# Sigmoid-gated layer behind routed attention: the values of the last batch in seven products of quarters

## The chip, the cores and the metric

The kernel runs on one core of a Trainium2 chip. The time is the device time of one execution in microseconds (us). Before the change the median of three runs is 320.71 us (320.22 to 320.73).

The engines go by the names of the profile: PE (TensorE, matrix products, with PEld for its weight loads), ACT (ScalarE), DVE (VectorE), POOL (GpSimd) and SP (the queue that issues most transfers). Each works off its own instructions in the order in which the program wrote them and waits at an instruction until what that one needs is there.

## The reference

Attention with routing, and then a gated layer on its output:

```python
mask = q_assign[:, :, :, None] == k_assign[:, :, None, :]
scores = np.where(mask, scale * np.matmul(q, k.transpose(0, 1, 3, 2)), -1000000000.0)
attn = np.exp(scores - np.max(scores, axis=-1, keepdims=True))
attn = attn / (np.sum(attn, axis=-1, keepdims=True) + 1e-09)
x = np.matmul(attn, v)                      # 4 batches, 8 heads, 768 tokens, 64
...                                         # heads side by side: 3072 x 512
gate = 1.0 / (1.0 + np.exp(-(x @ w_gate)))  # 512 x 1536
val = x @ w_val                             # 512 x 1536
out = gate * val @ w_out                    # 1536 x 512
```

q and k are assigned to the nearest of 16 centroids per head. Everything comes and goes as float32; the products run in float16 with float32 sums.

## The kernel before

**Attention.** The four batches follow each other. Each batch has 96 steps; a step is one product of scores (`sc`, line 1026), one exponential on ACT (`es`, 1031) and three small products with the values (`av`, 1049). The step counter runs from 0 to 383, and the last batch begins at step 288. A table `SCHED` gives for many small pieces of work the step at which they are written into the program. Between two steps `ffn_run` fills PE with the gated layer of the batch before, taken from a queue. So the layer of the last batch has no attention left to lie beside, and runs alone behind it: this is the stage that the change is about.

**Half inputs.** The attention puts 2.0 where the sum of the weights is formed, so the tile `xT` holds x / 2, transposed: four chunks of 128 columns (the contraction) by 768 tokens. With it, `1 + tanh(g)` is twice the sigmoid and the value group `v` is half of the value, and `(th + 1) * v` (line 643) is the gated value `hT`.

**Columns and blocks.** The 1536 columns of the layer are 12 groups of 128 (`fc`), the tokens of a batch two blocks of 384. A plain group (`fin_group`, 622) is four matmuls, one for each chunk.

**The last batch: `closing` (from line 646).** The groups 0 and 1 are plain, gate and value. The other ten are taken in pairs, by a `Unit` for each pair. For its gates a Unit doesn't compute four plain groups (two columns by two blocks, 16 matmuls) but seven products of quarters of two matmuls each (14): `p1` to `p7`. They need differences of the gate's weights (`fin_weights`, 602, eight of them, written at the steps in `SCHED["fw"]`) and of the tokens (`fin_tokens`, 616). Two PSUM banks hold the running sums of a Unit. `x` takes p1, then p6, p7 and p4 on top; after each of them ACT copies its state out (`c1` 693, `c12` 701, `c22` 710, and the tanh of `c21` 718). `y` takes p5 and later p3. DVE adds what is missing (`plus`, 650): p2 to `c1`, `y` to `c22`, and `y` with p3 to `c12`. ACT then takes the tanh in place (711, 719, 726). The next product into `x` cannot begin before the copy of the state before is done. The values of all ten groups are plain: four groups for each pair, 16 matmuls, and on DVE line 643 after each. They are written between the products of the next pair.

The order in `closing` is written out by hand in the list `seq`, and each engine keeps to it. Four PSUM banks are a pool called `ring` (plain groups and p2); a new tile gets the bank that was given back first. The pools `op` and `avp` have two banks each, for `x` and `y`. The second operands of the layer (`Sums.make`, 869 to 875) are sums over `hT` on DVE, and the tail of the stage is the output product, also by seven products (`pair`, 763), and its stores.

Of the kernel before, what the change touches and what calls it, by code (L numbers as in the profile page):

```python
# [8 lines left out]
FP = mybir.dt.float32  # L9
# [86 lines left out]
}  # L96


# [1 line left out]
def kernel(  # L100
# [61 lines left out]
    def bank(n=512, dt=FP, name="bank"):  # L162
        return ring.tile([128, n], dt, tag="ring", name=name)
# [3 lines left out]
    def out_bank():  # L167
        taken["op"] += 1
        return op.tile([128, DM], FP, tag="o", name="o")
# [225 lines left out]
    T = {}  # L395
# [187 lines left out]
                        "p (h x) -> p h x", h=2  # L583
                    )

    def fin_weights(i, t):

        fin_room()
        a = FC0 // 2 if i == 0 else 0
        q = lambda k, j: wg[i][:, 2 * k : 2 * k + 2].rearrange(  # L590
            "p d (q j) f -> p d q j f", j=2
        )[:, :, a:, j]
        tw = lambda t: fin["kq"[i], (t - 1) // 2][:, (t - 1) % 2].rearrange(
            "p (d q f) -> p d q f", d=2, q=3
        )
        fin["T", i, t] = tw(t)
# [5 lines left out]
        DVE.tensor_tensor(cut(z), cut(x), cut(y), ALU.subtract)  # L602
# [25 lines left out]
    def fin_plain(xT, fc, blk):  # L628
        b, st = B - 1, []

        def gate():
            if fc == 0:
                need(*(("x", b, p, 3 * blk + c) for p in range(NP) for c in range(3)))
                HB[b, blk] = htp.tile([128, NFC, 384], HP, name="hT")
            g = fin_group(xT, 0, fc, blk)
            st.append(thp.tile([128, 384], FP, name="th"))
            ACT.activation(st[0], g, AF.Tanh)

        return [(NDC * 163, gate), (NDC * 163, lambda: hidden(xT, fc, blk, st[0]))]

    def hidden(xT, fc, blk, th):
        w = fin_group(xT, 1, fc, blk)
        DVE.scalar_tensor_tensor(HB[B - 1, blk][:, fc], th, 1.0, w, ALU.add, ALU.mult)  # L643

    def closing(xT):

# [1 line left out]

        b = B - 1
        plus = lambda dst, a, z: DVE.tensor_tensor(dst, a, z, ALU.add)  # L650
        fin_tokens(xT, 4)
        room = [tp.tile([128, 12, 128], HP, tag="T", name="T") for _ in range(7)]
        slot = []
        for t in room[:4]:
# [4 lines left out]
        for m, n in ((m0, 0), (ma, 0), (mb, 1)):  # L659
            for i in (1, 2, 3):  # L660
                if n == 0:
                    m.of[i] = sump.tile([128, HF, 128], HP, tag="sum", name="sum")
                else:
                    m.of[i] = room[4 + i // 2][:, HF * (i % 2) : HF * (i % 2) + HF]
        m0.of[4], ma.of[4], mb.of[4] = room[4][:, 0:HF], room[6][:, 0:HF], room[6][:, HF:12]

        class Unit:
            def __init__(u, n, f):
                u.f, u.i, u.q = f, f // WQ, f % WQ // 2
                n = n % 2  # L670
                u.c1, u.c12, u.c22, u.c21 = slot[4 * n : 4 * n + 4]

            def mm(u, o, k, start, stop):
                T_ = lambda t, d: fin["T", u.i, t][:, d, u.q, :]
                W_ = lambda k_, j, d: wg[u.i][:, 2 * k_ + d, (u.f + j) % WQ, :]
                A_ = lambda i, k_, d: xT[:, 2 * k_ + d, 384 * (1 - i) : 384 * (2 - i)]
                S_ = lambda t, d: fin["S", t][:, d]
                for d in range(2):
                    l, r = {
                        1: lambda: (W_(0, 0, d), A_(0, 0, d)), 2: lambda: (W_(1, 0, d), A_(0, 1, d)),  # L680
                        3: lambda: (W_(1, 1, d), S_(4, d)), 4: lambda: (T_(4, d), A_(1, 1, d)),
                        5: lambda: (T_(1, d), S_(1, d)), 6: lambda: (T_(2, d), S_(2, d)),
                        7: lambda: (T_(3, d), S_(3, d)),
                    }[k]()
                    PE.matmul(  # L685
                        out=o, lhsT=l, rhs=r, start=start and d == 0, stop=stop and d == 1,
                        skip_group_check=True,
                    )

            def p1(u):  # L690
                u.x = out_bank()[:, 0:384]
                u.mm(u.x, 1, True, True)
                ACT.activation(u.c1, u.x, AF.Copy)

            def p5(u):
                u.y = avp.tile([128, 512], FP, tag="av", name="av")[:, 0:384]
                u.mm(u.y, 5, True, True)

            def p6(u):
                u.mm(u.x, 6, False, True)  # L700
                ACT.activation(u.c12, u.x, AF.Copy)

            def p2(u):
                z = bank(512, name="gz")[:, 0:384]
                u.mm(z, 2, True, True)
                plus(u.c1, z, u.c1)

            def p7(u):
                u.mm(u.x, 7, False, True)
                ACT.activation(u.c22, u.x, AF.Copy)  # L710
                ACT.activation(u.c1, u.c1, AF.Tanh)

            def sum22(u):
                plus(u.c22, u.y, u.c22)

            def p4(u):
                u.mm(u.x, 4, False, True)
                ACT.activation(u.c21, u.x, AF.Tanh)
                ACT.activation(u.c22, u.c22, AF.Tanh)

            def p3(u):
                u.mm(u.y, 3, False, True)
                plus(u.c12, u.y, u.c12)

            def tanh12(u):
                ACT.activation(u.c12, u.c12, AF.Tanh)
# [5 lines left out]
        seq = []  # L732
        units = [Unit(n, f) for n, f in enumerate((6, 2, 8, 4, 10))]
        old = [f for fc in range(FC0) for _, f in fin_plain(xT, fc, 1)]
        def part(i, m, c0, c1, eng=None):
            return lambda: m.make(i, c0, c1, eng)

        extra = {
            3: [part(3, m0, 0, 4), part(3, ma, 0, 4)],
            4: [part(1, m0, 0, 4), part(2, m0, 0, 4)],  # L740
        }
# [62 lines left out]
        u = units[-1]  # L804
        both = lambda m, *c: [part(1, m, *c), part(2, m, *c)]
        seq += [lambda: u.v(0), part(1, ma, 0, 4), u.p3, u.tanh12, p0(1), lambda: u.v(1), part(2, ma, 0, 4), pa(1)]
        seq += [lambda: u.v(2), *both(m0, 4, HF), pb(1), lambda: u.v(3), l0([(0, HD)]), *both(ma, 4, HF)]
        seq += [la([(0, HD)]), part(1, mb, 0, HF), p0(6), part(2, mb, 0, HF), p0(5)]
        seq += [part(3, m0, 4, HF), part(3, ma, 4, HF), pa(6), part(4, m0, 0, HF), pa(5), part(3, mb, 0, HF)]
        seq += [p0(7), part(4, ma, 0, HF), pb(6), part(4, mb, 0, HF), pb(5)]  # L810
        seq += [pa(7), p0(4), p0(3), pb(7), pa(4), pa(3), pb(4), pb(3), lb([(0, HD // 2), (HD // 2, HD)])]
        return [(0.0, f) for f in seq]

    def plain_out(b, blk, t):
# [847 lines left out]
    for b in range(B):  # L1662
        xT = xtp.tile([128, NDC, S], HP, tag="xTb", name="xTb")
        key = min(b, 1)
        for i in range(2 if b else NPT):
            u = BASE[b] + (DONE0[i] if b == 0 else 96 - 12 * halved(b) if i == 0 else 96)
            lag = SCHED.get(f"lag{key}{i}", 8)
            if b == B - 1:
                if i == 0:
                    at(u + lag, lambda xT=xT: queue.extend(a for fc in range(FC0) for a in fin_plain(xT, fc, 0)))  # L1670
                    at(u + SCHED.get("fs1", 9), lambda xT=xT: (fin_tokens(xT, 1), fin_tokens(xT, 2)))
                    at(BASE[b] + 48 + SCHED.get("fs3", 17), lambda xT=xT: fin_tokens(xT, 3))
                    for k, s_ in enumerate(SCHED["fw"]):
                        at(s_, lambda k=k: fin_weights(1 - k // 4, 1 + k % 4))
# [56 lines left out]
```

## Time and profile before

| | |
|---|---|
| median of the runs | 320.71 us |
| the profiled execution | 320.28 us |
| its span, first to last instruction | 318.5 us |
| PE busy over the span | 312.2 us (98%) |
| DVE, ACT, POOL busy | 233.7, 240.4 and 109.0 us |
| first matmul of the last batch's layer | 271.63 us |
| last matmul | 315.15 us |

Times in the views of the profile count from the first instruction. A row of the timeline gives the start, the duration, the engine, the line, the tiles written and read, and in brackets how long the engine was idle before it and what ended that. Matmuls are pipelined: a pair of them is shown with 0.49 us, though the next pair begins 0.33 us after it. A row of a group gives the count, the time in all and the mean of one in ns.

### The profile page before, as it was taken

What the parts mean: (1) busy time and instruction counts of PE and PEld (TensorE: products, weight loads), DVE (VectorE), ACT (ScalarE), POOL (GpSimd) and SP (SyncE); (2) the same over time, 40 slices, a digit from 0 to 9 for tenths busy, and PEclk for the clock granted to TensorE, in tenths of its full rate; (3) what the DMA queues carried; (4) which work ended last, traced back from release to release, by engine and by line L of the source; (5) the groups of instructions that cost most, each with busy time, mean ns of one, the idle gap of its engine ahead of it and who ended that gap; (6) DMA issues with size and microseconds to landing.
All of it is one profiled execution on the core that took longest, in us unless ns stands there. A gap on an engine that the chain in (4) does not pass through costs nothing.

```text
span 318.5 us, 9195 instructions
## 1 busy us (share of the span) xinstructions
PE 312.2 (98%) x3500; PEld 221.1 (69%) x3500; DVE 233.7 (73%) x615; ACT 240.4 (75%) x545; POOL 109.0 (34%) x145
## 2 busy tenths in 40 slices
PE   7999999999999999999999999999999999999995
PEld 5888666766766666666777678666777678666685
DVE  6899656778687777686779678776766777668873
ACT  6688998797889887877767786887878886466521
POOL 5888454244434275423233342523202111000000
PEclk9999999999999999999999999999999999999999
DMA  7999998748859988977775555872612120300014
GB/s 197 374 266 187 262 158 132 180 95 244 243 102 178 188 231 133 204 211 149 110 204 139 180 111 147 255 106 52 112 24 67 42 27 20 138 3 0 1 35 165
DMA packets 77996, 45.16 MB, mean 142 GB/s; under 512 B 56896, under 2 KB 75520, under 8 KB 77952
## 3 DMA queue, kind: packets, MB, share of 16 engines
q1 hardware_dynamic: 73840, 39.66, 51.3%
q0 software_dynamic: 3680, 4.72, 8.9%
q8 instruction: 27, 0.44, 0.6%
q10 hardware_dynamic: 432, 0.20, 0.2%
q14 instruction: 17, 0.14, 0.2%
HBM read 28.34 MB, written 6.29 MB: 109 GB/s over the span
## 4 chain that ended last, share of the span: by engine, by line
PE 95%; DVE 2%; POOL 1%; issue 0%; ACT 0%; POOLq 0%; DVEq 0%
PE sc L1026 19%; PE g L531 15%; PE v L547 15%; PE av L1049 11%; PE o L954 9%; PE v L622 5%; PE o L825 5%; PE lg L435 2%; PE o L685 2%; PE o_end L763 2%; PE lg L422 1%; PE o L763 1%; PE av L763 1%; PE av L685 1%; PE t_ps L1275 1%; PE oh_ps L1335 1%
## 5 line engine op out<-in xcount | busy, mean ns | idle before, releaser
L1031 ACT ACTIVATE es<-sc 128x384 f16<-128x384 f32 x384 | 174.1, 492 | 38.6 <-PE sc L1026 29.9
L1026 PE MATMUL sc<-T 128*128 128x384 f16 x384 | 117.5, 326 | 0.4 <-DVE T L1356 0.4
L1049 PEld LDWEIGHTS <-es 128*128 128x128 f16 x1152 | 81.3, 98 | 35.1 <-ACT es L1031 0.2
L1049 PE MATMUL av<-va,es 128*128 128x65 f16 x1152 | 97.6, 194 | 0.0
L552 DVE SCALAR_TENSOR_TENSOR hT<-th,v 128x384 f16<-128x384 f32 x72 | 39.8, 553 | 38.3 <-PE av L1049 34.1
L531 PE MATMUL g<-xTb,wg 128*128 128x384 f16 x288 | 58.5, 326 | 0.2 <-DVE hT L552 0.2
L547 PE MATMUL v<-xTb,wv 128*128 128x384 f16 x288 | 58.6, 326 | 0.1
L376 POOL TENSOR_TENSOR xp<-t,rec 128x384 f16<-128x384 f32 (+1 forms) x30 | 21.6, 721 | 96.9 <-DVE rec L373 48.1
L537 ACT ACTIVATE th<-g 128x384 f32<-128x384 f32 x72 | 35.4, 491 | 8.7 <-PE g L531 6.7
L531 PEld LDWEIGHTS <-wg 128*128 128x128 f16 x288 | 27.9, 97 | 14.3 <-issue 0.4
L547 PEld LDWEIGHTS <-wv 128*128 128x128 f16 x288 | 28.0, 98 | 13.9 <-issue 0.3
L1026 PEld LDWEIGHTS <-T 128*128 128x128 f16 x384 | 37.1, 97 | 0.7 <-DVE T L1356 0.7
L1592 POOL TENSOR_TENSOR hl<-kraw,hl 128x384 f16<-128x384 f32 x22 | 20.2, 920 | 41.4 <-DVE hl L1591 24.3
L1592 POOL TENSOR_TENSOR hl<-qraw,hl 128x384 f16<-128x384 f32 x22 | 21.2, 962 | 11.1 <-DVE hl L1591 11.1
L825 PE MATMUL o<-wo,hT 128*128 128x512 f16 x72 | 19.9, 379 | 0.0
L371 DVE TENSOR_TENSOR t<-av,sv 128x390 f32<-128x390 f32 (+1 forms) x30 | 14.4, 480 | 7.2 <-PE av L1049 5.2
L622 PE MATMUL v<-xTb,wv 128*128 128x384 f16 x96 | 18.9, 326 | 0.0
L901 DVE TENSOR_TENSOR ob<-o,ob 128x256 f32<-128x256 f32 (+1 forms) x28 | 15.0, 549 | 4.7 <-PE o L954 3.2
L954 PE MATMUL o<-wo,hT 128*128 128x256 f16 x108 | 16.8, 273 | 0.0
L954 PEld LDWEIGHTS <-sum 128*128 128x128 f16 x144 | 14.0, 97 | 3.3
L643 DVE SCALAR_TENSOR_TENSOR hT<-T,v 128x384 f16<-128x384 f32 x20 | 11.0, 552 | 5.3 <-PE v L622 5.3
L450 DVE TENSOR_REDUCE lgs<-lg 128x192 f32<-128x384 f32 x23 | 12.7, 551 | 2.3 <-PE lg L435 2.3
(207 smaller groups left out, 445.2 us busy)
## 6 DMA issues: line engine op xcount, KB each, us to landing
vraw<-in_v_dram SPq DMA_DIRECT2D x15, 384.0 KB, 5.0
kraw<-in_k_dram SPq DMA_DIRECT2D x14, 384.0 KB, 4.9
qraw<-in_q_dram SPq DMA_DIRECT2D x12, 384.0 KB, 4.1
out_dram<-ob SPq DMA_DIRECT2D x17, 256.0 KB, 2.2
wg<-in_moe_w_gate_dram POOLq DMA_DIRECT2D x2, 768.0 KB, 9.6
wv<-in_moe_w_val_dram POOLq DMA_DIRECT2D x2, 768.0 KB, 10.5
wo<-in_moe_w_out_dram POOLq DMA_DIRECT2D x2, 768.0 KB, 9.4
T<-ohT SPq DMA_DIRECT2D x44, 24.0 KB, 1.9
```

Source lines behind the costliest of these rows:

```text
L376: (eng or POOL).tensor_tensor(x, t[:, 0:nq, 0:64], bcast(rec[:, 0:nq], 64), ALU.mult)
L531: PE.matmul(out=g[:, 0:n], lhsT=wg[fc // WQ][:, dc, fc % WQ, :], rhs=xT[:, dc, t0 : t0 + n], start=(dc == 0), stop=(dc == NDC - 1),)
L537: ACT.activation(th[:, 0:n], g[:, 0:n], AF.Tanh)
L547: PE.matmul(out=w[:, 0:n], lhsT=wv[fc // WQ][:, dc, fc % WQ, :], rhs=xT[:, dc, t0 : t0 + n], start=(dc == 0), stop=(dc == NDC - 1),)
L552: DVE.scalar_tensor_tensor(HB[b, blk][:, fc, 0:n], st[0][:, 0:n], 1.0, w[:, 0:n], ALU.add, ALU.mult)
L622: PE.matmul(out=o[:, 0:384], lhsT=w[:, dc, fc % WQ, :], rhs=xT[:, dc, 384 * blk : 384 * blk + 384], start=(dc == 0), stop=(dc == NDC - 1),)
L825: PE.matmul(out=o, lhsT=HB[b, blk][:, fc, bass.ts(t, 128)], rhs=wo[fc // WON][:, fc % WON, :], start=(fc == 0), stop=(fc == NFC - 1),)
L954: PE.matmul(out=st[z][:, e], lhsT=a[:, c, :], rhs=rhs[:, c, :], start=start and c + e == 0, stop=c == HF - 1, skip_group_check=True,)
L1026: PE.matmul(out=sc.rearrange("p (c t) -> p c t", t=128), lhsT=s["k"], rhs=s["q"], start=True, stop=True,)
L1031: ACT.activation(es, sc, AF.Exp, scale=SCALE)
L1049: PE.matmul(out=av[:, a0 + s["c0"] + i, :], lhsT=s["es"][:, bass.ts(i, 128)], rhs=VA[b, p][:, e, s["j"], :], start=(first and i == 0 and a ...
L1592: POOL.tensor_tensor(hl[:, :, 64:128], r, hl[:, :, 0:64], ALU.subtract)
```

## The change

Four of the five pairs get their values by seven products of quarters as well, each between the gates of the next pair (pairs in the order 6, 2, 4, 8, 10; before 6, 2, 8, 4, 10). The values of the last pair, 10, stay plain.

- A value Unit costs 14 matmuls instead of 16. ACT copies its states `c12` and `c22` (times 2), DVE copies `c1` (times 2) and adds with `twice` (2a + z). The gated products of three of its quarters go to POOL (`gated`), the fourth is one DVE instruction straight from PSUM (in `p4`).
- It needs eight differences of the value weights; they are written at steps 328 to 345 into four tiles of the pool `hl`.
- The gates of the last batch are sigmoids of 2g in place of tanh, and the value is multiplied by 2. One instruction at the head of `closing` takes a sigmoid of a single column first. The other batches keep tanh.
- The `y` bank of a Unit comes from `ring` (the first Unit's from `avp`), the `x` of a value Unit from `avp`.
- The gate of `c12` of the pair before is written right behind its `p3`, ahead of `p6`; before, it stood behind `p6`.
- The plain gates and values of groups 0 and 1 in block 0 are now written at the head of `closing`, the token difference 4 behind them.
- The sums for the output products are dealt out anew: fewer beside the Units, more in the tail.

```diff
+    "fwv": [328, 328.5, 331.5, 332, 332.5, 340, 340.5, 345], "END": 0,
...
-            ACT.activation(st[0], g, AF.Tanh)
+            ACT.activation(st[0], g, AF.Sigmoid, scale=2.0)
...
     def hidden(xT, fc, blk, th):
         w = fin_group(xT, 1, fc, blk)
-        DVE.scalar_tensor_tensor(HB[B - 1, blk][:, fc], th, 1.0, w, ALU.add, ALU.mult)
+        DVE.scalar_tensor_tensor(HB[B - 1, blk][:, fc], w, 2.0, th, ALU.mult, ALU.mult)
...
+        twice = lambda dst, a, z: DVE.scalar_tensor_tensor(dst, a, 2.0, z, ALU.mult, ALU.add)
+        ACT.activation(r1, ones[:, 0:1], AF.Sigmoid)
+        first = [f for fc in range(FC0) for _, f in fin_plain(xT, fc, 0)]
+        seq = [*first, lambda: fin_tokens(xT, 4)]
...
+            def copy(u, dst):
+                ACT.activation(dst, u.x, AF.Copy, scale=2.0 if u.w else 1.0)
+
+            def gated(u, j, blk, z, th):
+                POOL.tensor_tensor(HB[b, blk][:, u.f + j], z, th, ALU.mult)
+
             def p1(u):
-                u.x = out_bank()[:, 0:384]
+                u.x = (avp.tile([128, 512], FP, tag="av", name="av") if u.w else out_bank())[:, 0:384]
                 u.mm(u.x, 1, True, True)
-                ACT.activation(u.c1, u.x, AF.Copy)
+                if u.w:
+                    DVE.tensor_scalar(u.c1, u.x, 2.0, None, ALU.mult)
+                else:
+                    u.copy(u.c1)
...
             def p2(u):
-                z = bank(512, name="gz")[:, 0:384]
+                z = bank(512, name="z")[:, 0:384]
                 u.mm(z, 2, True, True)
-                plus(u.c1, z, u.c1)
+                (twice if u.w else plus)(u.c1, z, u.c1)
+                if u.w:
+                    u.gated(0, 1, u.c1, u.g.c1)
...
             def sum22(u):
-                plus(u.c22, u.y, u.c22)
+                (twice if u.w else plus)(u.c22, u.y, u.c22)
+                if u.w:
+                    u.gated(1, 0, u.c22, u.g.c22)
 
             def p4(u):
                 u.mm(u.x, 4, False, True)
-                ACT.activation(u.c21, u.x, AF.Tanh)
-                ACT.activation(u.c22, u.c22, AF.Tanh)
+                if u.w:
+                    DVE.scalar_tensor_tensor(
+                        HB[b, 0][:, u.f], u.x, 2.0, u.g.c21, ALU.mult, ALU.mult
+                    )
+                else:
+                    ACT.activation(u.c21, u.x, AF.Sigmoid, scale=2.0)
 
             def p3(u):
                 u.mm(u.y, 3, False, True)
-                plus(u.c12, u.y, u.c12)
+                (twice if u.w else plus)(u.c12, u.y, u.c12)
+                if u.w:
+                    u.gated(1, 1, u.c12, u.g.c12)
...
-        for n, u in enumerate(units):
-            w = old if n == 0 else [lambda i=i, u=units[n - 1]: u.v(i) for i in range(4)]
-            l = units[n - 1] if n else None
-            ex = list(extra.get(n, []))
-            e = lambda k: [ex.pop(0) for _ in range(min(k, len(ex)))]
-            seq += [u.p1, w[0]] + ([l.p3] if l else []) + e(1) + [u.p5, u.p6]
-            seq += ([l.tanh12] if l else []) + [w[1], u.p2, u.p7, w[2], u.sum22]
-            seq += [w[3]] + e(1) + [u.p4]
+        for n in range(1, len(G)):
+            g, v, l = G[n], V[n - 1], G[n - 1]
+            seq += [
+                g.p1, v.p1, l.p3, lambda l=l: l.gate(l.c12), V[n - 2].p3 if n > 1 else none,
+                *extra.get(n, []), g.p6, g.p5, v.p6, g.p2, g.p7, g.sum22, v.p5, v.p7, v.sum22,
+                g.p4, v.p2, lambda g=g: g.gate(g.c1), v.p4, lambda g=g: g.gate(g.c22),
+            ]
...
-        seq += [lambda: u.v(0), part(1, ma, 0, 4), u.p3, u.tanh12, p0(1), lambda: u.v(1), part(2, ma, 0, 4), pa(1)]
...
+        seq += [
+            u.p3, lambda: u.gate(u.c12), V[-1].p3, p0(1), lambda: u.v(0), lambda: u.v(1), pa(1),
...
-                    at(u + lag, lambda xT=xT: queue.extend(a for fc in range(FC0) for a in fin_plain(xT, fc, 0)))
```

In the new list `G` are the Units of the gates, `V` those of the values; `l` is the pair before.

More of the change, by code (lines that the diff above doesn't have):

```diff
@@ L584, in fin_room, with fin_weights @@
                     )
-    def fin_weights(i, t):
+    def fin_weights(w, i, t):
         fin_room()
+        if w == 1 and ("h", 0) not in fin:
+            for n in range(4):
+                fin["h", n] = hlp.tile([128, 12, 128], HP, tag="hl", name="hl").rearrange(
+                    "p c x -> p (c x)"
+                ).rearrange("p (h x) -> p h x", h=2)
         a = FC0 // 2 if i == 0 else 0
-        q = lambda k, j: wg[i][:, 2 * k : 2 * k + 2].rearrange(
+        q = lambda k, j: (wg, wv)[w][i][:, 2 * k : 2 * k + 2].rearrange(
             "p d (q j) f -> p d q j f", j=2
         )[:, :, a:, j]
[L593 to L596, printed above, removed]
+        tw = lambda t: (fin["h", 2 * i + (t - 1) // 2] if w else fin["kq"[i], (t - 1) // 2])[
+            :, (t - 1) % 2
+        ].rearrange("p (d q f) -> p d q f", d=2, q=3)
+        fin["T", w, i, t] = tw(t)
         z, x, y = {
@@ L650, in closing @@
         plus = lambda dst, a, z: DVE.tensor_tensor(dst, a, z, ALU.add)
-        fin_tokens(xT, 4)
-        room = [tp.tile([128, 12, 128], HP, tag="T", name="T") for _ in range(7)]
+        twice = lambda dst, a, z: DVE.scalar_tensor_tensor(dst, a, 2.0, z, ALU.mult, ALU.add)
+        ACT.activation(r1, ones[:, 0:1], AF.Sigmoid)
+        first = [f for fc in range(FC0) for _, f in fin_plain(xT, fc, 0)]
+        seq = [*first, lambda: fin_tokens(xT, 4)]
         slot = []
-        for t in room[:4]:
+        for _ in range(8):
+            t = tp.tile([128, 12, 128], HP, tag="T", name="T")
             v = t.rearrange("p c x -> p (c x)").bitcast(FP)
@@ L658, in closing, with __init__ @@
         m0, ma, mb = sums.values()
-        for m, n in ((m0, 0), (ma, 0), (mb, 1)):
-            for i in (1, 2, 3):
-                if n == 0:
-                    m.of[i] = sump.tile([128, HF, 128], HP, tag="sum", name="sum")
-                else:
[L664 to L671, printed above, removed]
+        vs_ = []
+        for _ in range(3):
+            t = rawp.tile([128, 2, NCH, 64], FP, tag="vraw", name="vraw", bufs=3)
+            t = t.rearrange("p a c d -> p (a c d)").bitcast(HP).rearrange("p (c x) -> p c x", x=128)
+            vs_ += [t[:, 0:HF], t[:, HF:12]]
+        for m in (m0, ma):
+            for i in (1, 2, 3):
+                m.of[i] = sump.tile([128, HF, 128], HP, tag="sum", name="sum")
+        mb.of[1], mb.of[2], mb.of[3], m0.of[4], ma.of[4], mb.of[4] = vs_
+        class Unit:
+            def __init__(u, w, n, f):
+                u.w, u.f, u.i, u.q = w, f, f // WQ, f % WQ // 2
+                if w:
+                    u.c1, u.c12, u.c22 = slot[3 * (n % 2) : 3 * (n % 2) + 3]
+                else:
+                    u.c22, u.c21 = slot[6 + 2 * (n % 2) : 8 + 2 * (n % 2)]
+                    u.c1, u.c12 = slot[10 + 2 * (n % 3) : 12 + 2 * (n % 3)]
             def mm(u, o, k, start, stop):
-                T_ = lambda t, d: fin["T", u.i, t][:, d, u.q, :]
-                W_ = lambda k_, j, d: wg[u.i][:, 2 * k_ + d, (u.f + j) % WQ, :]
+                T_ = lambda t, d: fin["T", u.w, u.i, t][:, d, u.q, :]
+                W_ = lambda k_, j, d: (wg, wv)[u.w][u.i][:, 2 * k_ + d, (u.f + j) % WQ, :]
                 A_ = lambda i, k_, d: xT[:, 2 * k_ + d, 384 * (1 - i) : 384 * (2 - i)]
@@ L730, in v, with part @@
                 hidden(xT, u.f + j, blk, th)
[L732 to L741, printed above, removed]
-        for n, u in enumerate(units):
-            w = old if n == 0 else [lambda i=i, u=units[n - 1]: u.v(i) for i in range(4)]
-            l = units[n - 1] if n else None
-            ex = list(extra.get(n, []))
-            e = lambda k: [ex.pop(0) for _ in range(min(k, len(ex)))]
-            seq += [u.p1, w[0]] + ([l.p3] if l else []) + e(1) + [u.p5, u.p6]
-            seq += ([l.tanh12] if l else []) + [w[1], u.p2, u.p7, w[2], u.sum22]
-            seq += [w[3]] + e(1) + [u.p4]
+        def part(i, m, c0=0, c1=HF):
+            return lambda: m.make(i, c0, c1)
+        FS = (6, 2, 4, 8, 10)
+        G = [Unit(0, n, f) for n, f in enumerate(FS)]
+        V = [Unit(1, n, f) for n, f in enumerate(FS[:-1])]
+        for g, v in zip(G, V):
+            v.g = g
+        u = G[0]
+        w = [f for fc in range(FC0) for _, f in fin_plain(xT, fc, 1)]
+        seq += [
+            u.p1, w[0], lambda u=u: u.p5(avp.tile([128, 512], FP, tag="av", name="av")), u.p6, w[1],
+            u.p2, u.p7, lambda u=u: u.gate(u.c1), w[2], u.sum22, w[3], u.p4, lambda u=u: u.gate(u.c22),
+        ]
+        none = lambda: None
+        extra = {3: [part(1, m0, 0, 2)], 4: [part(2, m0, 0, 2), part(3, m0)]}
+        for n in range(1, len(G)):
[4 more added lines that the diff above has]
+                g.p4, v.p2, lambda g=g: g.gate(g.c1), v.p4, lambda g=g: g.gate(g.c22),
+            ]
         def pair(m, bk):
@@ L1669 @@
                 if i == 0:
-                    at(u + lag, lambda xT=xT: queue.extend(a for fc in range(FC0) for a in fin_plain(xT, fc, 0)))
                     at(u + SCHED.get("fs1", 9), lambda xT=xT: (fin_tokens(xT, 1), fin_tokens(xT, 2)))
                     at(BASE[b] + 48 + SCHED.get("fs3", 17), lambda xT=xT: fin_tokens(xT, 3))
-                    for k, s_ in enumerate(SCHED["fw"]):
-                        at(s_, lambda k=k: fin_weights(1 - k // 4, 1 + k % 4))
+                    for w in range(2):
+                        for k, s_ in enumerate(SCHED["fw" + "gv"[w]]):
+                            at(s_, lambda k=k, w=w: fin_weights(w, 1 - k // 4, 1 + k % 4))
                 continue
```

28 lines of the change are left out of this document (14 added, 14 removed), and 2 rows, old and new, of the table SCHED.

## The prediction

> **What bounds the kernel now.** First the page: busy shares and granted clock.
>
> ```profile
> span 318.5 us, 9195 instructions
> PE 312.2 (98%) x3500; PEld 221.1 (69%) x3500; DVE 233.7 (73%) x615; ACT 240.4 (75%) x545; POOL 109.0 (34%) x145
> PEclk9999999999999999999999999999999999999999
> ```
>
> PE is the bound, at full clock. The stage of the change lies at the end of the span, so next the busy times by stretch (PE, PEld, DVE, ACT, POOL in this order; then clock, DMA share, GB/s), two of the Units and two of the tail:
>
> ```profile
> 280.00:285.00 5.00, 5.00 (x33) 3.00 (x32) 3.58 (x8) 3.31 (x8) 0.00 (x0) 1.00 0.00 2
> 290.00:295.00 5.00, 5.00 (x32) 3.03 (x31) 4.32 (x10) 3.20 (x8) 0.00 (x0) 1.00 0.00 0
> 300.00:305.00 5.00, 5.00 (x42) 3.91 (x41) 4.06 (x12) 1.56 (x4) 0.00 (x0) 1.00 0.00 0
> 305.00:310.00 5.00, 5.00 (x48) 4.47 (x47) 4.09 (x11) 1.61 (x5) 0.00 (x0) 1.00 0.17 56
> ```
>
> PE is busy all of the time: here each matmul less is time less, and each wait of PE that arises is time more, one to one. DVE and ACT have a third to an eighth of their time free. The timeline of PE gives the period: p1 of the second and of the fourth pair (line 685, a pair of matmuls), the p6 of the second, and the first plain value behind the last pair.
>
> ```profile
> 278.78 0.49 PE L685 MATMUL o<-xTb,wg 128*128 128x384 f16 x2
> 280.41 0.49 PE L685 MATMUL o<-kraw 128*128 128x384 f16 x2
> 288.53 0.49 PE L685 MATMUL o<-xTb,wg 128*128 128x384 f16 x2
> 298.28 0.81 PE L622 MATMUL v<-xTb,wv 128*128 128x384 f16 x4
> ```
>
> Two pairs take 288.53 - 278.78 = 9.75 us, one 4.88 us, which is 14 + 16 = 30 matmuls of 0.1625 us; four pairs end at 298.28 on the same beat. So PE waits for nothing now. A product of two matmuls takes 0.325 us of PE, and its result is there 0.49 us after its start.
>
> **The saving.** Four pairs get their values with 14 matmuls, not 16: 8 x 0.1625 = 1.30 us less PE time. Nothing else leaves PE. The plain groups of block 0 ran at 271.63, behind the attention, already; writing them in `closing` moves nothing on PE. On SP no transfer is added or moved.
>
> **What it costs, in the pairs.** Of one pair in the new order: ACT has nine instructions (three copies and four gates of the gate Unit, two copies of the value Unit; before seven), DVE eight (3 `plus`, 3 `twice`, the copy of `c1`, the fourth gated product; before seven), POOL three. Their sizes from the timelines of ACT and DVE and from the groups by form:
>
> ```profile
> 279.37 0.51 ACT L719 ACTIVATE T<-T 128x384 f32<-128x384 f32 x1
> 279.78 0.48 ACT L693 ACTIVATE T<-o 128x384 f32<-128x384 f32 x1
> 280.93 0.49 ACT L701 ACTIVATE T<-o 128x384 f32<-128x384 f32 x1 [0.67 <-PE o L685]
> 281.32 0.51 ACT L726 ACTIVATE T<-T 128x384 f32<-128x384 f32 x1
> 300.63 0.52 ACT L726 ACTIVATE T<-T 128x384 f32<-128x384 f32 x1 [1.25 <-DVE T L650]
> 282.88 0.56 DVE L643 SCALAR_TENSOR_TENSOR hT<-T,v 128x384 f16<-128x384 f32 x1 [0.21 <-PE v L622]
> 283.35 0.55 DVE L650 TENSOR_TENSOR T<-av,T 128x384 f32<-128x384 f32 x1
> 283.82 0.55 DVE L643 SCALAR_TENSOR_TENSOR hT<-T,v 128x384 f16<-128x384 f32 x1
> 300.04 0.55 DVE L650 TENSOR_TENSOR T<-av,T 128x384 f32<-128x384 f32 x1
> ```
>
> An instruction of ACT takes 0.49 us, and the next in line begins 0.40 us after it (279.37, 279.78; 280.93, 281.32); on DVE 0.55 us and 0.47 us (282.88, 283.35, 283.82). From the end of a product to ACT pass 0.03 us (280.41 + 0.49 to 280.93), from DVE to ACT 0.04 us (300.04 + 0.55 to 300.63). Nine times 0.40 is 3.6 us and eight times 0.47 is 3.8 us, both under the 28 x 0.1625 = 4.55 us of PE. So neither engine is full; what decides is the order. From an engine back to a waiting product, one row pair from early in the span:
>
> ```profile
> 32.71 0.55 DVE L1356 COPY T<-oh_ps 16x768 f16<-16x768 f16 x1
> 33.32 0.34 PE L1026 MATMUL sc<-T 128*128 128x384 f16 x1 [0.38 <-DVE T L1356]
> ```
>
> 0.06 us (33.26 to 33.32).
>
> Now the wait that the change adds. The gate of `c12` of the pair before (`l.gate`) is written ahead of `g.p6`, so on ACT it stands in front of the copy of `c12` of the new pair, and `g.p7` cannot start before that copy is done. While ACT waits at the gate, the copies of `c12` of both Units stand behind it, and on PE everything behind `g.p7`. The gate itself waits for the `plus` of `l.p3` on DVE, and ahead of that `plus` DVE has, in order, `twice` of `c22`, `twice` of `c1`, the fourth gated product and the copy of `c1` of the next value Unit. The first of these waits for `v.p7`, two products behind the `g.p7` of the pair before. That closes a loop from one `g.p7` to the next:
>
> - `v.p7` starts 2 x 0.325 = 0.65 us later, its result is there at 1.14; ACT copies from 1.17 to 1.66.
> - DVE from 1.70: five instructions in a row, 4 x 0.47 + 0.55 = 2.43, to 4.13. Their products (`v.p2`, `v.p4`, the next `v.p1` and `l.p3`, within 3.3 us) are there by then.
> - ACT: the gate from 4.17, the copy of `c12` 0.40 later, from 4.57 to 5.06.
> - PE: `g.p7` at 5.06 + 0.06 = 5.12 us.
>
> PE has 4.55 us of matmuls for that round, so it waits 0.57 us in each, at `g.p7` and (0.11 of it) at `g.p4`: the copy of `c22` is done 0.49 + 0.03 + 0.49 + 0.06 = 1.07 us behind the start of `g.p7`, and only three products (0.98 us) lie between. There are three such rounds: 1.71 us.
>
> The first round has no earlier value Unit, but `g.p6` comes three products behind `g.p1` where it came five behind: at 278.78 + 0.98 = 279.76. The copy that it needs started at 279.78 (row L693 above), behind the gates of the first pair, which the change leaves ahead of it; it ends at 280.26, PE goes on at 280.32: 0.56 us. With the 0.11 at `g.p4`, 0.67 us.
>
> Sum: 0.67 + 1.71 - 1.30 = +1.08 us.
>
> What the price of the new forms does: the copy of `c1` on DVE (a tensor_scalar from PSUM) has no row of its size, `twice` only its kin L643. The nearest rows:
>
> ```profile
> L347 DVE TENSOR_SCALAR sv<-vs_ps 128x130 f32<-128x130 f32 x12 | 3.4, 283 | 0.6 <-PE vs_ps L342 0.6
> ```
>
> It reads a third of the columns in 0.28 us, so the new one lies between 0.28 and 0.55; I take 0.55 (0.47 as a step), as all DVE rows of 384 columns from PSUM have it. At the low end each round is 0.19 shorter, 0.57 us in all. At the high end no start on DVE overlaps the instruction before: 4 x 0.08 a round, +0.96 us. That end is also what the Trainium skill says in "VectorE: DVE Perf Modes", "The DRAIN you can't avoid": the next op does not start until the pipe is empty, though it allows ops that start earlier. By it the sum would be +2.0 us; the starts 0.47 us apart above speak for its exception, and I stay with 0.47.
>
> **What lies beside other work.** POOL: 12 gated products of two float32 tiles. Nearest rows, with the DVE instructions that ran beside one:
>
> ```profile
> L1592 POOL TENSOR_TENSOR hl<-kraw,hl 128x384 f16<-128x384 f32 x22 | 20.2, 920 | 41.4 <-DVE hl L1591 24.3
> 247.31 0.82 POOL L376 TENSOR_TENSOR xp<-t,rec 128x384 f16<-128x384 f32 x1 [6.41 <-issue]
> 247.19 0.56 DVE L552 SCALAR_TENSOR_TENSOR hT<-th,v 128x384 f16<-128x384 f32 x1
> 247.66 0.88 DVE L873 TENSOR_TENSOR sum<-hT 128x768 f16<-128x768 f16 x1
> ```
>
> 0.82 to 0.92 us each, under 2.8 us a round of 5.1; the first reader of what it writes is a sum one pair later. POOL has nothing else there (0.00 in the stretches above). It would bind only beyond 1.5 us each. Beside POOL, L873 with both inputs in SBUF took 0.88 us, 0.33 more than the 0.55 of L602 at the same size (next fence); L552, which reads PSUM, stayed at 0.56. All five instructions of the loop read PSUM, so I add nothing.
>
> The eight differences of the value weights go to DVE under the attention. The group of the matmul of line 1026 from 229.8 us on counts 57, so that is step 327 of 384, and from 242.3 on 40, step 344: the window of steps 328 to 345.
>
> ```profile
> L1026 PE MATMUL sc<-T x57: 323/325/327, 229.8 to 268.9; 128*128 128x384 f16 x57
> L1026 PE MATMUL sc<-T x40: 324/326/327, 242.3 to 268.9; 128*128 128x384 f16 x40
> L602 DVE TENSOR_TENSOR qraw<-wg 128x768 f16<-128x768 f16 x2 | 1.1, 552 | 0.0
> L602 DVE TENSOR_TENSOR kraw<-wg,kraw 128x512 f16<-128x512 f16 x2 | 1.1, 572 | 0.0
> 231.44 0.55 DVE L552 SCALAR_TENSOR_TENSOR hT<-th,v 128x384 f16<-128x384 f32 x1 [1.47 <-PE av L1049]
> 234.71 0.56 DVE L552 SCALAR_TENSOR_TENSOR hT<-th,v 128x384 f16<-128x384 f32 x1 [1.91 <-PE av L1049]
> 241.00 0.55 DVE L552 SCALAR_TENSOR_TENSOR hT<-th,v 128x384 f16<-128x384 f32 x1 [1.27 <-PE av L1049]
> 243.97 0.56 DVE L552 SCALAR_TENSOR_TENSOR hT<-th,v 128x384 f16<-128x384 f32 x1 [0.75 <-PE av L1049]
> ```
>
> Two fall at step 328, three at 331.5 to 332.5, two at 340, one at 345: at most 1.1, 1.7, 1.1 and 0.57 us, and DVE stood idle 1.47, 1.91, 1.27 and 0.75 us just there. Nothing added; without that cover a late L552 would hold a bank of `ring`, 0.3 us each time, some 1 us.
>
> The sigmoid needs another activation table. Its load has a row from the lead-in, and ACT's gap behind the attention has two:
>
> ```profile
> L1502 ACT ACT_TABLE_LOAD x1 | 1.3, 1283 | 0.0
> 268.74 1.07 ACT L1031 ACTIVATE es<-sc 128x384 f16<-128x384 f32 x2 [0.42 <-PE sc L1026]
> 272.48 0.49 ACT L637 ACTIVATE th<-g 128x384 f32<-128x384 f32 x1 [2.67 <-PE g L622]
> ```
>
> 1.28 us fit into 2.67 idle; uncovered it would cost at most that. The tail gets its sums later, about 0.6 us more DVE work (0.55 + 2 x 0.28 done beside the pairs where 4 x 0.42 were), into some 0.9 us free in each 5: nothing; uncovered 0.6.
>
> **The rivals.** *The saving shows.* It needs rounds that close within PE's 4.55 us, 0.57 shorter: DVE's five starts 0.33 us apart, or less. Then only the first pair waits: 0.67 - 1.30 = -0.63; and -1.30 if that one is hidden too. 319.4 to 320.1 us. For it speaks that no engine is full, against it each row of the loop. *It about cancels*: rounds of 4.65 to 4.95 us (DVE's copy of `c1` at its low end, waits shorter than the one pair shows), 320.2 to 321.2. *POOL slows the loop's DVE work*: its two products follow `twice` of `c22` and of `c1`, just beside the next three DVE instructions. At 0.33 us each (L873) that is +1.0 a round, +3.0, 324.8 us. The Trainium skill, "SBUF — State Buffer", "Who interferes with whom", has a DVE instruction with two SBUF inputs contend with GpSimd, one with at most one not; L873 and L552 agree with it. *DVE without overlap*, or the weight differences in the way: about +2.0, 322.8 us.
>
> **How the numbers follow.** The profiled execution takes 320.28 us around its span of 318.5: 320.28 + 1.08 = 321.4. It lies 0.43 under the median of 320.71, to which the forecast goes: 320.71 + 1.08 = 321.8 us, by itself 321.2 to 322.8 with the two ends of DVE. Chances: the forecast 0.50, cancelled 0.17, the saving 0.18, POOL 0.05, the +2.0 cases 0.10. A change within 0.2% (0.64 us) is about what a measurement of this kernel cannot tell from none: faster 0.18, same 0.17, slower 0.65. The range runs from 319.8, in the middle of the saving, to 323.0, above the +2.0; half of the saving and POOL's case, 0.14, stay outside.
>
> **What would show it.** Right: the waits of PE name `g.p7` behind the ACT copy of `c12`, 0.4 to 0.6 us in three pairs, and `g.p6` once; p1 to p1 about 5.1 us; one more table load before 272; PE without a wait before 271 and in the tail. Wrong: p1 to p1 at 4.6 us, POOL products beyond 1.5 us, DVE instructions at 0.88 in the loop, or waits on L552 at 230 to 244.

## The result and the profile after

The changed kernel takes 322.08 us (median of 13 runs, 321.36 to 323.75), the kernel before 320.68 us beside it. The ratio is 1.0049 with a 95% interval of 1.0029 to 1.007: slower by 0.5%, 1.40 us between the medians. The profiled execution of the changed kernel took 322.44 us.

The page of the changed kernel, busy shares, and the waits of PE from 222 us to the end:

```profile
span 320.6 us, 9224 instructions
PE 312.7 (98%) x3492; PEld 220.6 (69%) x3492; DVE 239.2 (75%) x623; ACT 244.9 (76%) x555; POOL 121.3 (38%) x157
```

```profile
PE o L699 <- ACT T L705: 1.2, 4, 0.4
PE g L532 <- DVE hT L553: 0.2, 1, 0.2
```

PE has 3492 matmuls instead of 3500: the saving is there. Behind it stand waits where before there was none: four times the chain of `x` (line 699 is now the line of the Units' matmuls, 705 that of their copies on ACT), and once a plain gate group under the attention (532, 553). The shown waits are shorter than what PE loses, since a pair of matmuls is drawn with 0.49 us where the next begins 0.325 us after it.

The timeline of PE, the first and the last matmul of the stage, each p1 of the gate Units, each product that waited for line 705, the products around the waits of the third pair, and the p3 of the last pair:

```profile
272.73 0.81 PE L628 MATMUL g<-xTb,wg 128*128 128x384 f16 x4
279.88 0.49 PE L699 MATMUL o<-xTb,wg 128*128 128x384 f16 x2
281.42 0.48 PE L699 MATMUL o<-kraw 128*128 128x384 f16 x2 [0.39 <-ACT T L705]
284.78 0.49 PE L699 MATMUL o<-xTb,wg 128*128 128x384 f16 x2
287.05 0.49 PE L699 MATMUL z<-xTb,wg 128*128 128x384 f16 x2
287.84 0.48 PE L699 MATMUL o<-qraw,kraw 128*128 128x384 f16 x2 [0.30 <-ACT T L705]
288.49 0.49 PE L699 MATMUL av<-qraw,hl 128*128 128x384 f16 x2
288.96 0.49 PE L699 MATMUL o<-xTb,kraw 128*128 128x384 f16 x2
289.93 0.49 PE L699 MATMUL o<-xTb,wg 128*128 128x384 f16 x2
292.93 0.48 PE L699 MATMUL o<-qraw 128*128 128x384 f16 x2 [0.23 <-ACT T L705]
295.03 0.49 PE L699 MATMUL o<-xTb,wg 128*128 128x384 f16 x2
298.03 0.48 PE L699 MATMUL o<-qraw 128*128 128x384 f16 x2 [0.23 <-ACT T L705]
300.12 0.49 PE L699 MATMUL y<-qraw,wg 128*128 128x384 f16 x2
316.47 0.83 PE L800 MATMUL o_end<-wo,hT 128*128 128x128 f16 x12
```

From p1 to p1 the second pair takes 4.90 us, the third 5.15, the fourth 5.10, and the fifth, up to the next product behind it, 5.09. Within the third, the product behind 287.05 should start 0.325 us later, at 287.38; it starts at 287.84: 0.46 us lost at `g.p7`. `g.p4` starts at 288.96 where 288.49 + 0.325 = 288.81 was its turn: 0.15. At the `g.p7` of the fourth and the fifth pair, 292.93 and 298.03, the same working gives 0.40 us each; from one `g.p7` to the next are 5.09 and 5.10 us. In the second pair `g.p6` starts at 281.42, not three products behind its p1, at 279.88 + 0.98 = 280.86: 0.56 us.

The loop itself in that third pair, from the timelines of DVE and ACT:

```profile
284.44 0.56 DVE L657 SCALAR_TENSOR_TENSOR T<-y,T 128x384 f32<-128x384 f32 x1
284.91 0.55 DVE L657 SCALAR_TENSOR_TENSOR T<-z,T 128x384 f32<-128x384 f32 x1
285.38 0.55 DVE L745 SCALAR_TENSOR_TENSOR hT<-av,T 128x384 f16<-128x384 f32 x1
285.84 0.55 DVE L714 TENSOR_SCALAR T<-av 128x384 f32<-128x384 f32 x1
286.30 0.55 DVE L656 TENSOR_TENSOR T<-y,T 128x384 f32<-128x384 f32 x1
286.88 0.52 ACT L758 ACTIVATE T<-T 128x384 f32<-128x384 f32 x1 [0.86 <-DVE T L656]
287.31 0.47 ACT L705 ACTIVATE T<-o 128x384 f32<-128x384 f32 x1
```

Five instructions of DVE in a row, 0.47 us apart; the last is the `plus` of `c12`. ACT stands idle for 0.86 us at the gate of `c12` (758), and behind it waits the copy (705) that `g.p7` needs: 287.31 + 0.47 = 287.78, and PE starts at 287.84.

The stage from its first to its last matmul, by the start of the last row, is 316.47 - 272.73 = 43.74 us. Before, by these two rows of its timeline, it was 314.31 - 271.63 = 42.68 us:

```profile
271.63 0.81 PE L622 MATMUL g<-xTb,wg 128*128 128x384 f16 x4
314.31 0.83 PE L763 MATMUL o_end<-wo,hT 128*128 128x128 f16 x12
```

So the stage is 1.06 us longer. The rest of the spans' difference of 2.1 us comes earlier, and is of two kinds. Scores of step 327 and of the last step, 383, before and after:

```profile
229.77 0.32 PE L1026 MATMUL sc<-T 128*128 128x384 f16 x1
268.90 0.32 PE L1026 MATMUL sc<-T 128*128 128x384 f16 x1
```

```profile
230.53 0.33 PE L1064 MATMUL sc<-T 128*128 128x384 f16 x1
270.01 0.32 PE L1064 MATMUL sc<-T 128*128 128x384 f16 x1
```

Up to step 327 the changed kernel's execution lies 0.76 us back, though the change writes nothing there. In the eight profiles of the experiments below that moment lies between 229.6 and 231.2 us, in no order that goes with the edits: it differs from execution to execution. From step 327 to 383 it is 39.13 us before and 39.48 after, 0.35 us more, and this stays the same wherever the weight differences stay where the change put them (39.46 to 39.48 in four profiles; 39.12 or 39.13 in the three where they are written earlier). 1.06 + 0.35 = 1.41 us, beside 1.40 between the medians. The interval of the ratio leaves 0.9 to 2.2 us for that difference, so an agreement this close is in part luck.

### The profile page after: what moved, and what is told of

It is laid out like the page before. It is cut to its first block, busy times and chain, and to the rows that moved or that the text cites. A ratio compares the mean times of both kernels' runs of the same rounds, so it can differ in the third digit from the quotient of the medians.

```text
span 320.6 us, 9224 instructions
## 1 busy us (share of the span) xinstructions
PE 312.7 (98%) x3492; PEld 220.6 (69%) x3492; DVE 239.2 (75%) x623; ACT 244.9 (76%) x555; POOL 121.3 (38%) x157
## 4 chain that ended last, share of the span: by engine, by line
PE 91%; DVE 3%; DMA 2%; ACT 2%; issue 1%; POOL 0%; SPq 0%; DVEq 0%
PE sc L1064 18%; PE g L532 15%; PE v L548 15%; PE av L1087 10%; PE o L992 8%; PE o L863 4%; PE lg L436 2%; PE o L699 2%; PE o_end L800 2%; PE y L699 2%; PE av L699 2%; PE v L628 1%; DMA T<-hl 1%; PE av L800 1%; PE o L800 1%; PE lg L423 1%
## 5 line engine op out<-in xcount | busy, mean ns | idle before, releaser
L548 PE MATMUL v<-xTb,wv 128*128 128x384 f16 x288 | 58.6, 326 | 0.1
L708 POOL TENSOR_TENSOR hT<-T 128x384 f16<-128x384 f32 x12 | 12.2, 1033 | 17.5 <-DVE T L657 16.3
L324 POOL CAST va<-vraw 128x768 f16<-128x768 f32 x15 | 13.3, 886 | 1.8 <-DMA vraw<-in_v_dram 1.8
```

Of the source, the lines that this page charges most:

```text
L548: PE.matmul(out=w[:, 0:n], lhsT=wv[fc // WQ][:, dc, fc % WQ, :], rhs=xT[:, dc, t0 : t0 + n], start=(dc == 0), stop=(dc == NDC - 1),)
```

## The experiments

Where a run has one time only, the stretches of the profile carry the verdict: p1 to p1, the stage from the first to the last matmul, and steps 327 to 383. These single times, in the order of the text, are 324.39, 322.95, 321.51, 321.61, 321.66 and 323.49 us; beside the last four the kernel before took 321.10 us once.

**The gate behind the copy.** One instruction moves on ACT.

```diff
-                g.p1, v.p1, l.p3, lambda l=l: l.gate(l.c12), V[n - 2].p3 if n > 1 else none,
-                *extra.get(n, []), g.p6, g.p5, v.p6, g.p2, g.p7, g.sum22, v.p5, v.p7, v.sum22,
+                g.p1, v.p1, l.p3, V[n - 2].p3 if n > 1 else none,
+                *extra.get(n, []), g.p6, lambda l=l: l.gate(l.c12), g.p5, v.p6, g.p2, g.p7, g.sum22, v.p5, v.p7, v.sum22,
```

> One instruction of ACT per pair moves: the gate of c12 of the pair before stands behind the copy of c12 that g.p6 feeds, no longer ahead of it. Work on every engine stays the same. Theory 'the order on ACT closes the loop': g.p7 no longer depends on DVE, its wait of about 0.46 us in the pairs 3, 4 and 5 is gone, p1 to p1 there falls from 5.10 to about 4.67 us (what is left is 0.11 at g.p4), the wait at g.p6 of the second pair (0.56) stays; 3 x 0.45 = 1.4 us less than the changed kernel, about the time of the kernel before or 0.1 to 0.3 us above it where the weight differences under the attention cost 0.33. Rival 'DVE is too full, with eight instructions and the sums': its work is the same, so p1 to p1 stays at 5.1 us and the time at that of the changed kernel. Rival 'POOL's three products hold the pairs up': the same, 5.1 us.

320.58 us beside 320.42 for the kernel before, ratio 1.001 (0.9997 to 1.0024). The p1 of the pairs 2 to 5 in its timeline of PE, with the one wait that is left between them:

```profile
280.54 0.49 PE L699 MATMUL o<-xTb,wg 128*128 128x384 f16 x2
282.08 0.48 PE L699 MATMUL o<-kraw 128*128 128x384 f16 x2 [0.40 <-ACT T L705]
285.41 0.49 PE L699 MATMUL o<-xTb,wg 128*128 128x384 f16 x2
290.11 0.49 PE L699 MATMUL o<-xTb,wg 128*128 128x384 f16 x2
294.81 0.49 PE L699 MATMUL o<-xTb,wg 128*128 128x384 f16 x2
```

4.70 us from p1 to p1 (4.55 and the 0.15 at `g.p4`), the wait at `g.p7` gone, the stage 42.47 us: 1.27 us less with the same work on every engine. That is 0.21 under the kernel before in the stage; with the 0.35 of steps 327 to 383, 0.14 above it, beside 0.16 measured. DVE was not too full, and POOL held up nothing; the place of one instruction in ACT's order did.

**One instruction more on DVE, inside the loop and beside it.** Inside, the copy of `c1` is made twice:

```diff
                     DVE.tensor_scalar(u.c1, u.x, 2.0, None, ALU.mult)
+                    DVE.tensor_scalar(u.c1, u.x, 2.0, None, ALU.mult)
```

> The copy of c1 of each value Unit is made twice on DVE, 0.47 us more per pair, at a place inside the loop (ahead of the plus of l.p3). Theory 'loop': each round grows by all of it, p1 to p1 from 5.10 to 5.57 us in the pairs 3 to 5, some 1.4 us in all. Rival 'DVE is too full': also longer by up to 0.47 a pair, so this run tells only beside the next one.

p1 to p1 was 5.74 us and 5.69 us in the third and fourth pair, the stage 46.10 us. The loop grew by 0.59 rather than 0.47: the second copy, which writes the tile of the first, began 0.58 us behind it (286.04, 286.62).

The first attempt to put the same size beside the loop:

```diff
+            def idle(u):
+                DVE.tensor_scalar(
+                    thp.tile([128, 384], FP, name="th"), u.x, 2.0, None, ALU.mult
+                )
...
-                *extra.get(n, []), g.p6, g.p5, v.p6, g.p2, g.p7, g.sum22, v.p5, v.p7, v.sum22,
+                *extra.get(n, []), g.p6, g.p5, v.p6, v.idle, g.p2, g.p7, g.sum22, v.p5, v.p7, v.sum22,
```

> The same instruction of the same size on DVE (a scaled copy from the bank x of the value Unit), but into a spare tile and behind v.p6, where DVE waits for the copies of ACT anyway and nothing of the loop stands behind it. Theory 'loop': p1 to p1 stays at 5.10 us. Rival 'DVE is too full': 5.10 + 0.47 = 5.57 us, as with the extra instruction inside the loop.

That was a miss: 5.42 us, 0.32 more than in the changed kernel. The timelines of DVE and PE show why.

```profile
287.79 0.56 DVE L758 TENSOR_SCALAR th<-av 128x384 f32<-128x384 f32 x1 [0.89 <-ACT T L705]
288.40 0.48 PE L699 MATMUL av<-qraw,hl 128*128 128x384 f16 x2 [0.17 <-DVE th L758]
```

The added instruction reads the bank `x` behind ACT's copy of the same bank, and waited for it 0.89 us; `v.p7` writes that bank, so it waited for the added instruction, and `v.p7` is part of the loop. It was not beside the loop. So a second attempt, with a bank that nobody waits for:

```diff
                 (twice if u.w else plus)(u.c1, z, u.c1)
+                if not u.w:
+                    DVE.tensor_scalar(
+                        thp.tile([128, 384], FP, name="th"), z, 2.0, None, ALU.mult
+                    )
```

> One instruction more on DVE for each gate Unit, 0.47 us, reading the bank of p2 a second time behind its plus, into a spare tile. Nothing of the loop reads or writes that bank, and DVE stood idle there for 0.75 us. Theory 'loop': p1 to p1 in the pairs 3 to 5 stays at 5.10 us. Rival 'DVE is too full': 5.5 us or so, as with the extra instruction inside the loop.

```profile
283.85 0.49 PE L699 MATMUL o<-xTb,wg 128*128 128x384 f16 x2
289.01 0.49 PE L699 MATMUL o<-xTb,wg 128*128 128x384 f16 x2
294.11 0.49 PE L699 MATMUL o<-xTb,wg 128*128 128x384 f16 x2
```

5.16 and 5.10 us, the stage 43.75 us beside 43.74: five instructions more on DVE cost nothing. With the run inside the loop this settles it for the changed kernel: what counts here is not how much DVE does but what stands ahead of the `plus` of `c12`.

**The same place in the kernel before.** No value Units, no sigmoids, only the order:

```diff
-            seq += [u.p1, w[0]] + ([l.p3] if l else []) + e(1) + [u.p5, u.p6]
-            seq += ([l.tanh12] if l else []) + [w[1], u.p2, u.p7, w[2], u.sum22]
+            seq += [u.p1, w[0]] + ([l.p3, l.tanh12] if l else []) + e(1) + [u.p5, u.p6]
+            seq += [w[1], u.p2, u.p7, w[2], u.sum22]
```

> The kernel before, tanh and plain values as they were, with one thing of the change: the tanh of c12 of the pair before stands ahead of p6, so on ACT ahead of the copy of c12. Theory 'that place holds up g.p7': the plus that it waits for ended 2.27 us behind p1 (p1 at 283.66, line 650 at 285.38 for 0.55), the tanh starts at 2.31, the copy at 2.71, and p7 can start at 3.26 where it came at 2.93: 0.33 us of waiting in each of four pairs, p1 to p1 5.2 us in place of 4.88, 1.3 us in all. Rival 'the place does no harm by itself, only the value Units do': 4.88 us.

```profile
284.02 0.49 PE L685 MATMUL o<-xTb,wg 128*128 128x384 f16 x2
287.28 0.48 PE L685 MATMUL o<-qraw 128*128 128x384 f16 x2 [0.17 <-ACT T L701]
289.22 0.49 PE L685 MATMUL o<-xTb,wg 128*128 128x384 f16 x2
294.43 0.49 PE L685 MATMUL o<-xTb,wg 128*128 128x384 f16 x2
```

5.20 and 5.21 us from p1 to p1 instead of 4.88 (5.13 in the second pair), the stage 43.91 us, 1.23 more: as forecast. The place does harm by itself; what stands ahead of the `plus` is another chain here than in the changed kernel, since there are no value Units.

**The weight differences earlier.**

```diff
-    "fwv": [328, 328.5, 331.5, 332, 332.5, 340, 340.5, 345], "END": 0,
+    "fwv": [327.5, 327.5, 328, 328.5, 331.5, 340, 340.5, 345], "END": 0,
```

> Of the changed kernel only the steps of the eight differences of the value weights change: the first five half a step to a step earlier, so that two fall into the idle 1.47 us of DVE ahead of the gated value at 232.2 us and the fifth no longer stands behind the choice of the centroids. Theory 'the fifth difference pushed the gated value by 0.36 us, and a bank of the ring came free too late': the wait of a plain gate group of PE at 239.7 us is gone, and from step 327 to the first matmul of the last layer the program takes 0.33 us less than in the changed kernel; everything else stays. Rival 'the rest of the delay ahead of the stage (some 0.76 us before step 328, where the program is the same) comes from the change too, over the transfers': it stays as it is, or moves with these differences.

Steps 327 and 383 in its timeline:

```profile
230.10 0.32 PE L1064 MATMUL sc<-T 128*128 128x384 f16 x1
269.23 0.32 PE L1064 MATMUL sc<-T 128*128 128x384 f16 x1
```

39.13 us, as before the change, and no wait of a plain group; the stage stayed at 43.75. So the 0.35 us belong to the differences. The rival falls by the profiles taken together: with the differences where the change put them, step 327 came at 229.62 us in one run (the second beside the loop) and at 231.20 in another (the gate behind the copy), here at 230.10, so the 0.76 us are not theirs.

**The gated products on DVE.** In the version of the next experiment, one word:

```diff
-                POOL.tensor_tensor(HB[b, blk][:, u.f + j], z, th, ALU.mult)
+                DVE.tensor_tensor(HB[b, blk][:, u.f + j], z, th, ALU.mult)
```

> The version without waits (orders changed, weight differences earlier), with the three gated products of each value Unit on DVE in place of POOL. DVE then has eleven instructions a pair, 11 x 0.47 = 5.2 us, over PE's 4.55. Theory 'loop' and common sense: p1 to p1 rises from 4.55 to at least 5.2 us, 2 us or more in all, so POOL's share is needed and costs nothing where it is. Rival 'POOL's products hold the pairs up': 4.55 us or less waiting than now.

p1 to p1 5.74 us, PE waiting for the copy of `c1` (line 714) in three pairs, the stage 45.74 us against 41.53. Here DVE is indeed too full: it was busy 5.60 of 5.70 us between 289.00 and 294.70. The round is longer than the 5.2 us of eleven instructions at 0.47, in part because each gated product, which reads what the instruction ahead of it wrote, started 0.58 or 0.59 us behind that one (289.19 behind 288.61, 290.26 behind 289.67). POOL's share is worth 4.2 us, and the version with it (next) has no wait left for it to cause in the pairs 3 to 5.

**A version that beats both.** Order alone, and the weight differences as above:

```diff
-            u.p2, u.p7, lambda u=u: u.gate(u.c1), w[2], u.sum22, w[3], u.p4, lambda u=u: u.gate(u.c22),
+            u.p2, u.p7, lambda u=u: u.gate(u.c1), w[2], u.sum22, w[3], u.p4,
...
-                g.p1, v.p1, l.p3, lambda l=l: l.gate(l.c12), V[n - 2].p3 if n > 1 else none,
-                *extra.get(n, []), g.p6, g.p5, v.p6, g.p2, g.p7, g.sum22, v.p5, v.p7, v.sum22,
-                g.p4, v.p2, lambda g=g: g.gate(g.c1), v.p4, lambda g=g: g.gate(g.c22),
+                g.p1, *([lambda l=l: l.gate(l.c22)] if n == 1 else []), v.p1, l.p3,
+                V[n - 2].p3 if n > 1 else none, *extra.get(n, []), g.p6, v.p6,
+                lambda l=l: l.gate(l.c12), g.p5, g.p2, g.p7, g.sum22, v.p7, v.p5, v.sum22,
+                lambda g=g: g.gate(g.c1), v.p2, g.p4, v.p4, lambda g=g: g.gate(g.c22),
```

> All the waits that the theory names are taken away by order alone: the products of both Units stand four places apart in each chain (p1, p6, p7, p4), the gate of c12 behind both copies of c12, in the second pair the gate of c22 of the first pair behind the copy of c1, and the first five weight differences half a step to a step earlier, into the idle 1.47 us of DVE ahead of the line that they pushed. Theory 'loop': p1 to p1 4.55 us in the pairs 3 to 5, 0.2 us of waiting left in the second, no wait of the gate groups under the attention; 8 x 0.1625 = 1.30 us saved less 0.2: about 1.1 us or 0.35% under the kernel before, 2.5 us under the changed one. Rival 'DVE is too full' or 'POOL holds the pairs up': waits move to another product and the time stays above the kernel before.

319.2 us beside 320.42 for the kernel before: ratio 0.9967 (0.9955 to 0.998). Its p1 in the timeline of PE:

```profile
278.81 0.49 PE L699 MATMUL o<-xTb,wg 128*128 128x384 f16 x2
283.19 0.49 PE L699 MATMUL o<-xTb,wg 128*128 128x384 f16 x2
287.74 0.49 PE L699 MATMUL o<-xTb,wg 128*128 128x384 f16 x2
292.29 0.49 PE L699 MATMUL o<-xTb,wg 128*128 128x384 f16 x2
```

4.55 us, the 28 matmuls and nothing else; 4.38 in the second pair, 26 matmuls (4.23) and 0.15 of waiting; the stage, from 271.66 to 313.19, 41.53 us, 1.15 under the kernel before, of the 1.30 that the matmuls are worth. This run changes several places at once; what each is worth by itself is shown only for the gate of `c12` and for the differences, by the runs above.

## Why the prediction was right, point by point

- **The saving.** 8 matmuls, 1.30 us: there, and reached but for 0.15 us by the version that beats both.
- **The loop.** Forecast 5.12 us a round, measured 5.15, 5.10 and 5.09 from p1 to p1; at `g.p7` 0.46 forecast, 0.46, 0.40 and 0.40 measured; at `g.p4` 0.11 forecast (its terms, 1.07 - 0.975, give 0.10), 0.15 measured. The loop sets the round, so what PE waits at `g.p4` it does not wait at the next `g.p7`: 0.15 and 0.40 make 0.55, beside 0.57 forecast. Moving the gate, lengthening the loop, the second attempt to lengthen beside it, and the gate at the same place in the kernel before went as the mechanism says; the first attempt beside the loop was not beside it. So the mechanism is shown.
- **The second pair.** 0.67 us of waiting forecast, and 4.90 - 4.23 = 0.67 measured, 0.56 of it at `g.p6`.
- **The sum.** +1.08 us forecast for the stage, +1.06 measured. The forecast time of 321.8 us fell short by 0.3, and that has one place:
- **The weight differences, costed at nothing, cost 0.35 us.** The step that failed is the cover. I set the idle time of DVE ahead of each gated value against the work, but an instruction that is written behind others runs behind them. Rows of DVE, and the group of PE behind them:

```profile
232.20 0.55 DVE L553 SCALAR_TENSOR_TENSOR hT<-th,v 128x384 f16<-128x384 f32 x1 [1.47 <-PE av L1087]
235.47 0.56 DVE L553 SCALAR_TENSOR_TENSOR hT<-th,v 128x384 f16<-128x384 f32 x1 [0.39 <-PE av L1087]
235.94 0.55 DVE L608 TENSOR_TENSOR hl<-wv,hl 128x768 f16<-128x768 f16 x1
237.95 0.42 DVE L608 TENSOR_TENSOR hl<-wv 128x512 f16<-128x512 f16 x1
239.09 0.55 DVE L553 SCALAR_TENSOR_TENSOR hT<-th,v 128x384 f16<-128x384 f32 x1
239.69 0.81 PE L532 MATMUL g<-xTb,wg 128*128 128x384 f16 x4 [0.17 <-DVE hT L553]
```

  The 1.47 us that I gave to the two differences of step 328 are idle as before: they ran behind the gated value at 232.20, at 233.14 and 233.72, and with the third, at 234.54, filled most of the 1.91 us meant for the next three. The fourth (235.94) and the fifth (237.95, behind the choice of the centroids) came behind the gated value at 235.47, where those 1.91 us end. Ahead of the next gated value, at 239.09, the kernel before had 0.37 us idle, too little for both; it came 0.36 us late (3.62 us behind the one at 235.47, 3.26 before the change). The run with the first five written earlier shows that their place was the cause; it does not separate the fourth from the fifth.
  The price without cover, 0.3 us for a late gated value, was the right size, though the prediction shows no working for it, and L552 (now 553) between 230 and 244 us was named as a sign.
- **The new forms.** The copy of `c1` from PSUM (L714) took 0.55 us and `twice` 0.55, with starts 0.47 us apart: the ends of 0.28 us and of no overlap both fell. "VectorE: DVE Perf Modes" of the Trainium skill, "The DRAIN you can't avoid", has the next op wait until the pipe is empty, except for one that is not held; the starts 0.47 us apart of instructions of 0.55 us follow its exception, not its rule.
- **POOL.** 12 products of 1.03 us on average, not 0.82 to 0.92, with no effect on the pairs 3 to 5 (4.55 us a round with them in the version that beats both):

```profile
285.07 1.96 POOL L708 TENSOR_TENSOR hT<-T 128x384 f16<-128x384 f32 x2 [11.53 <-DVE T L657]
```

  The instructions of DVE beside it (285.38, 285.84, 286.30 above) stayed at 0.55 us, so the rival of contention fell. "SBUF — State Buffer" of the Trainium skill, "Who interferes with whom", says that a DVE instruction with at most one input in SBUF does not contend with GpSimd; these three are of that kind, and the trace agrees. One product on POOL took 1.39 us (at 297.65) in place of 1.00, while DVE ran a sum with both inputs in SBUF (297.62).
- **The table load.** One more, hidden as forecast: it ended at 272.21, before the first gate matmul (272.73), and ACT still stood idle 1.15 us until that group was done.

```profile
270.93 1.28 ACT L658 ACT_TABLE_LOAD   x1
```

- **The tail.** No wait of PE in it, as forecast. The 0.6 us more of sums on DVE did not come: the sums written behind the pairs took 5.8 us, before the change 5.9, though more columns are summed there. They are written in larger pieces: 768 columns at once took 0.55 us, 512 and 256 apart 0.42 and 0.29.

## What to carry to other kernels

Where PE is full, add up the round that leads from one product through the other engines back to the next such product, with what stands ahead of each step in its engine's order; compare it with PE's time for the round. No engine needs to be full for that round to bind: here one gate ahead of one copy cost 1.3 us, and an instruction of DVE beside the loop cost nothing. Idle time of an engine covers new work only if that work is written ahead of what ends the idle time.

## What had not been expected

Two readers of one bank went one behind the other: in the first attempt beside the loop, the added read on DVE started only when ACT's copy of the same bank was done (287.27 + 0.48, start at 287.79). Whether the chip or the program's own waits ask for that was not tried. Differences of two tiles in SBUF took about twice their time beside an instruction of POOL: in the run with the weight differences earlier, one L608 at 768 columns (230.77, POOL busy from 230.42 for 0.99 us) needed 1.06 us, the others 0.53 to 0.55. And the time that an execution needs up to step 327, where the programs do not differ, varied over 1.6 us between profiles, more than the change itself is worth; stretches of the trace tell the parts of such a change where spans cannot.
